# A last network in scaled float16 parts for passes 2 to 4, its last steps held behind the next pair of experts, and a planner that models port and clock

## The chip, the cores and the metric

The kernel runs on one core of one Trainium2 chip. The metric is device time in microseconds (us), from launch to end. The program gives each engine its own stream of instructions, in a written order: TensorE (PE) multiplies matrices, with weight loads shown apart as PEld; VectorE (DVE), ScalarE (ACT) and GpSimd (POOL) work element by element; SyncE (SP) issues most DMAs.

## The reference, cut to what matters

Three networks follow one another, all in float32; float64 stands for no output, but the last network's weights arrive as float64 words.

```python
a = softmax(where(sink or in window, q @ k.T / 8, -1e9)) @ v     # 2 x 8 heads, 768 positions, 64 wide
x = a as 1536 tokens x 512

flat = (x @ w_gate).flatten()                  # 8 experts, room for 192 tokens each
for idx in argsort(-flat):                     # greedy: best pair first
    tok, e = idx // 8, idx % 8
    if not taken[tok] and counts[e] < 192: assign tok to e
out[mask_e] = maximum(x[mask_e] @ w1[e], 0) @ w2[e]     # 512 -> 1024 -> 512, per expert

h = out @ w_in                                 # 512 -> 2048
g = maximum(h, 0) + alpha * minimum(h, 0)
return g @ w_out                               # 2048 -> 512
```

## The kernel before, in words

Attention runs first, to about 115 us of the profiled span. The greedy assignment then runs in eight phases, s = 0 to 7. Each fills one expert: comparisons `cm` on DVE and ACT (L994, L998, L1003), counts on PE (`closing`, L1045), and the list of that expert's 192 tokens. Between phases the tokens still free are packed closer (`compact`: a prefix count on PE, L1154 and L1156, then scatters `cd` on POOL, L1180, and a load back into a shorter table L). A gather on POOL (`xg`, L1295) fetches each expert's token rows, PE turns them (L1308), and the expert's two layers run as products in float32 (L1369), with weights `raw` loaded from memory.

Experts are taken in four pairs. After pair g comes pass g of the last network over that pair's 384 tokens: sixteen steps f = 0 to 15. A step multiplies the tokens by one 512 x 128 tile of w_in (`lay1`, L1423, 384 columns), applies the leaky rectifier (t on ACT, L1436; v on DVE, L1439), and multiplies by one 128 x 512 tile of w_out (`lay2`, L1458, 3 x 512 columns). A float32 operand is held as a high and a low part of type fp32r (a rounded float32 word). Three products, high x high, high x low, low x high, are summed: 12 matmuls in `lay1`, 9 in `lay2`. `split` makes the two parts of a weight tile (high on ACT, L1333; low on DVE, L1324), and does it again in each pass that uses the tile; x and g are split too (L1399, L1401; L1443, L1324). The first three steps of pass 1 are plain float32 (`FLAT1`, `FLAT2`; L1429). The text counts passes from 1, the code counts g from 0.

The 32 weight tiles come as pairs of 32-bit words and are turned into float32 during pair 1 and pass 1 (`Weights.convert`: ACT L796, DVE L798 and L800, then a sign from ACT L804 multiplied in on POOL L807). They stay in SBUF. A pass ends with an eviction from PSUM (L1492) and a scatter of its rows to `out` by POOL (L1496).

The order on every engine is written by `Plan`, a list scheduler. Each task carries an estimated duration; a task's rank is its longest way to the end. The planner takes what can start first by its own clock, with rank to break ties, and so decides before the run how phases, experts and passes are interleaved. The order is then fixed, whatever happens on the chip.

Of the kernel before, what the change touches and what calls it, by code (L numbers as in the profile page):

```python
# [74 lines left out]
class Task:  # L75
    __slots__ = ("eng", "fn", "deps", "succ", "left", "start", "end", "rank", "bufs", "tail", "n", "behind", "nbytes", "est", "by", "boost", "pre", "bias")


class Plan:
# [3 lines left out]
    HOP, SAME, BIAS = 0.2, 0.06, 0.85  # L83

    def __init__(self):
        self.tasks, self.soft, self.free = [], [], {}
        self.dma_free = 0.0

    def task(self, eng, fn, r=(), w=(), behind=None, after=(), tail=0.0, boost=0.0, nbytes=0, pre=None, bias=None):
# [3 lines left out]
        t = Task()  # L93
        t.eng, t.fn, t.tail, t.boost, t.n = eng, fn, tail, boost, len(self.tasks)
        deps = set(after)
# [36 lines left out]

    def run(self):
# [20 lines left out]
        while count:  # L154
            best = None
            for e, c in ready.items():
                at = self.free.get(e, 0.0)
                pick = None
                for t in c:
                    s, asked = max(at, t.est[e]), []  # L160
# [25 lines left out]
            self.free[e] = s + t.eng[e]  # L186
# [552 lines left out]
class Weights:  # L739


    LATE = 6

    def __init__(self, tc, nc, plan, ctx, w_in, w_out, alpha, wide, early):
# [4 lines left out]
        self.x, self.res, self.order, self.tasks = {}, {}, [None], []  # L749
        self.room(ctx, 0, early)  # L750
        cst = ctx.enter_context(tc.tile_pool(name="w_al", bufs=1))
        al, self.way, self.slope = [cst.tile([128, FB], F32, name=n) for n in ("al", "way", "slope")]
        al_res, self.way_res = Res(), Res()

# [10 lines left out]
    def room(self, ctx, a, b):  # L765
        pool = ctx.enter_context(self.tc.tile_pool(name=f"w_cst{a}", bufs=1))
        for n in range(a, b):
            self.x[n] = pool.tile([128, DM], F32, name=f"w{n}")
            self.res[n] = Res()

    def convert(self, a, b):
        nc, plan = self.nc, self.plan
        for n in range(a, b):
            f, s = divmod(n, 2)
            src, x, res = self.src[s][:, f], self.x[n], self.res[n]
            if not self.wide:
                plan.task({"SP": 0.06}, lambda x=x, src=src: nc.sync.dma_start(out=x, in_=src), w=[res],
                          nbytes=1 << 18)
                if s:
                    self.tasks.append(plan.task({"DVE": dve(DM // 2)}, lambda x=x, f=f: nc.vector.tensor_scalar(  # L780
                        x, x, self.way[:, f:f + 1], None, OP.mult), r=[self.way_res], w=[res]))
# [10 lines left out]
            def bits(k, r=r, x=x, sg=sg, f=f, s=s):  # L792
                lo, hi = words(r)[:, :, 0], words(r)[:, :, 1]
                b = x.bitcast(U32)
                if k == 0:
                    nc.scalar.activation(x, hi.bitcast(F32), AF.Copy, scale=2.0 ** -112)  # L796
# [9 lines left out]
            def signed(e, x=x, sg=sg):  # L806
                (nc.gpsimd if e == "POOL" else nc.vector).tensor_tensor(x, x, sg.tile, OP.mult)  # L807
# [3 lines left out]
            self.tasks.append(plan.task({"DVE": dve(DM // 2)}, lambda f=bits: f(1), w=[res]))  # L811
            plan.task({"DVE": dve(DM)}, lambda f=bits: f(2), r=[r], w=[res])
            if apart:
                plan.task({"ACT": act_sb(DM)}, lambda f=bits: f(4), r=[r, self.way_res] if s else [r], w=[sg])
                self.tasks.append(plan.task({"POOL": pool(DM), "DVE": dve(DM)}, signed, r=[sg], w=[res]))
            else:
                self.tasks.append(plan.task({"DVE": dve(DM)}, lambda f=bits: f(3), r=[r], w=[res]))
# [21 lines left out]
class Routed:  # L839
# [6 lines left out]
    LEAD = 0  # L846
# [73 lines left out]

    def name(self, ei, k, x, key):
# [8 lines left out]
    def closing(self, s, st, groups, r_bank, hold=(), fetched=False):  # L930
# [15 lines left out]
        for a, b in groups:  # L946
# [12 lines left out]
            if fetched:  # L959
# [4 lines left out]
                     r=[m.part(a)], w=[ps], after=hold)  # L964
# [5 lines left out]
            for x in range(a, b, 4) if not fetched else ():  # L970
# [11 lines left out]
                task({"PE": 0.11 * k}, bcast, r=[m.part(a)], w=[ps], after=hold)  # L982
# [5 lines left out]
            for a1, b1 in done:  # L988
                for c1 in range(a1, b1):
# [39 lines left out]
                    for k, x, y, op in sides:  # L1029
# [9 lines left out]
                        seq.append(task({"DVE": us}, fn, r=() if via else rr, w=cut[-1:]))  # L1039
                    counted.append(cnt.part(len(counted)))  # L1040

                    def count(c1=c1, cm=cm, lo=lo, b=b):
                        begun.append(c1)
                        for c in range(lo, b):
# [5 lines left out]
                         after=hold)  # L1050
# [24 lines left out]
        seq.append(task({"PE": 0.12}, lambda: total(0), r=[red, *counted], w=[cnt.part("t")]))  # L1075
        seq.append(task({"DVE": 0.25}, lambda: total(1), r=[cnt.part("t")], w=[tot]))
        seq.append(task({"PE": 0.12}, lambda: total(2), r=[tot], w=[cnt.part("b")]))
# [17 lines left out]
    def build(self, ctx, w1, w2, weights, out):  # L1095
# [23 lines left out]
        weights.r64.more(wrk, self.MORE)  # L1119
# [478 lines left out]
```

## Time and profile before

| | us |
|---|---|
| median of 3 runs | 651.32 (649.09 to 655.09) |
| profiled execution, whole | 645.53 |
| profiled execution, span | 643.8 |
| PE busy in it | 592.1 (92%) |
| PE weight loads | 510.5 (79%) |
| DVE busy | 399.0 (62%) |
| ACT busy | 321.0 (50%) |
| POOL busy | 172.8 (27%) |

The span runs from the first to the last instruction. A busy PE is counted from the start of a matmul to its modelled end, so steps overlap; the time that a matmul costs in a dense run is from its start to the next one's start. The mean granted TensorE clock is 0.962 of full speed. Passes and pairs of the profiled execution lie as follows: pass 1 to about 285 us, pair 2 to 333, pass 2 to 407, pair 3 to 453, pass 3 to 524, pair 4 to 571, pass 4 to 636, and the last stores to 644.

### The profile page before, as it was taken

What the parts mean: (1) busy time and instruction counts of PE and PEld (TensorE: products, weight loads), DVE (VectorE), ACT (ScalarE), POOL (GpSimd) and SP (SyncE); (2) the same over time, 40 slices, a digit from 0 to 9 for tenths busy, and PEclk for the clock granted to TensorE, in tenths of its full rate; (3) what the DMA queues carried; (4) which work ended last, traced back from release to release, by engine and by line L of the source; (5) the groups of instructions that cost most, each with busy time, mean ns of one, the idle gap of its engine ahead of it and who ended that gap; (6) DMA issues with size and microseconds to landing.
All of it is one profiled execution on the core that took longest, in us unless ns stands there. A gap on an engine that the chain in (4) does not pass through costs nothing.

```text
span 643.8 us, 11469 instructions
## 1 busy us (share of the span) xinstructions
PE 592.1 (92%) x4227; PEld 510.5 (79%) x4228; DVE 399.0 (62%) x1112; ACT 321.0 (50%) x670; POOL 172.8 (27%) x257
## 2 busy tenths in 40 slices
PE   6689996589799988989999999999999998999995
PEld 3466775359697777869999987899998888999994
DVE  4798999889578999863026587500656830035551
ACT  5688887345467885431225544311554441235552
POOL 4676726153384442131024011210000121000001
PEclk9999998569899999989999999999999999999998
DMA  7966344156887630516510005464000336600001
GB/s 216 278 132 134 98 85 129 57 203 205 319 271 226 202 130 1 176 53 212 180 49 5 0 25 182 147 193 135 26 2 0 135 104 190 202 1 1 1 1 49
DMA packets 41216, 76.53 MB, mean 119 GB/s; under 512 B 16324, under 2 KB 23016, under 8 KB 41064
## 3 DMA queue, kind: packets, MB, share of 16 engines
q1 hardware_dynamic: 38376, 68.87, 35.1%
q0 software_dynamic: 2784, 6.93, 3.2%
q8 instruction: 33, 0.54, 0.4%
q14 instruction: 23, 0.19, 0.1%
HBM read 66.75 MB, written 6.42 MB: 114 GB/s over the span
## 4 chain that ended last, share of the span: by engine, by line
PE 64%; DVE 15%; DMA 11%; issue 3%; POOL 3%; ACT 2%; SPq 1%; POOLq 0%; DVEq 0%; ACTq 0%
PE h L1369 19%; PE o L1458 16%; PE h L1423 16%; DMA xg<-xd,sidx 4%; PE s L459 3%; DVE cm L998 2%; PE pt L494 2%; DMA xT<-x 2%; DMA vraw<-v 2%; PE r L1308 2%; DVE spl L1324 2%; POOL cd L1180 2%; DVE w L798 1%; DVE w L800 1%; DVE cm L1013 1%
## 5 line engine op out<-in xcount | busy, mean ns | idle before, releaser
L1458 PE MATMUL o<-spl,gt 128*128 128x512 f32 x549 | 141.6, 400 | 0.9 <-DVE gt L1324 0.9
L1423 PE MATMUL h<-x,spl 128*128 128x384 f32 x732 | 138.0, 338 | 1.2 <-DVE spl L1324 1.2
L1423 PEld LDWEIGHTS h<-x,spl 128*128 128x128 f32 x732 | 128.3, 188 | 6.8 <-DVE spl L1324 1.5
L1324 DVE TENSOR_TENSOR spl<-w,spl 128x512 fp32r<-128x512 f32 x121 | 87.3, 722 | 55.3 <-ACT spl L1333 55.1
L1333 ACT CAST spl<-w 128x512 fp32r<-128x512 f32 x122 | 75.5, 619 | 87.3 <-PE o L1458 49.7
L1458 PEld LDWEIGHTS o<-spl,gt 128*128 128x128 f32 x549 | 101.0, 190 | 20.5 <-DVE gt L1324 1.5
L1369 PE MATMUL h<-xT,raw 128*128 128x192 f32 x512 | 91.7, 336 | 0.0
L1369 PEld LDWEIGHTS h<-xT,raw 128*128 128x128 f32 x512 | 85.3, 195 | 0.7 <-ACT h L1383 0.3
L1369 PE MATMUL h<-h,raw 128*128 128x192 f32 x512 | 85.8, 327 | 0.0
L1369 PEld LDWEIGHTS h<-h,raw 128*128 128x128 f32 x512 | 83.2, 190 | 0.3 <-issue 0.2
L1401 DVE TENSOR_TENSOR x<-h,x 128x192 fp32r<-128x192 f32 x32 | 11.3, 356 | 102.1 <-ACT x L1399 101.9
L1295 POOL DMA_INDIRECT xg<-xd,sidx x16 | 19.6, 1225 | 165.3 <-DVE sidx L1291 122.7
L1383 ACT ACTIVATE h<-h 128x192 f32<-128x192 f32 x64 | 21.1, 330 | 55.3 <-PE h L1369 55.3
L480 ACT ACTIVATE P<-sm,mn 128x260 f32<-128x260 f32 (+1 forms) x96 | 43.0, 490 | 8.1 <-DVE mn L469 7.3
L1439 DVE SCALAR_TENSOR_TENSOR v<-h,way,t 128x384 f32<-128x384 f32 x61 | 37.2, 611 | 12.8 <-ACT t L1436 12.8
L1436 ACT ACTIVATE t<-h,slope 128x384 f32<-128x384 f32 x64 | 37.0, 579 | 14.9 <-PE h L1423 14.2
L469 DVE CUSTOM_DVE_ANT_0 sm<-s,mask 128x260 f32<-128x260 f32 (+1 forms) x96 | 35.4, 398 | 8.4 <-PE s L459 7.5
L807 POOL TENSOR_TENSOR w<-w,sg 128x512 f32<-128x512 f32 x23 | 29.6, 1289 | 40.5 <-DVE w L800 22.1
L1443 ACT CAST gt<-v 128x384 fp32r<-128x384 f32 x61 | 31.1, 511 | 17.9 <-DVE v L1439 16.5
L459 PE MATMUL s<-k,q 64*128 64x260 f32 (+1 forms) x192 | 35.0, 455 | 4.7 <-DMA q<-qT 4.7
L998 DVE TENSOR_SCALAR cm<-mrow,m 128x384 bf16<-128x384 f32 (+8 forms) x75 | 37.3, 535 | 1.1 <-ACT mrow L983 1.1
L1399 ACT CAST x<-h 128x192 fp32r<-128x192 f32 x32 | 10.3, 322 | 53.8 <-PE h L1369 53.8
(207 smaller groups left out, 845.4 us busy)
## 6 DMA issues: line engine op xcount, KB each, us to landing
raw<-w SPq DMA_DIRECT2D x64, 512.0 KB, 3.8
r<-w_in SPq DMA_DIRECT2D x16, 512.0 KB, 3.6
r<-w_out SPq DMA_DIRECT2D x16, 512.0 KB, 3.7
vraw<-v SPq DMA_DIRECT2D x4, 768.0 KB, 11.5
xd<-x SPq DMA_DIRECT2D x12, 256.0 KB, 2.0
k<-kT SPq DMA_DIRECT2D x11, 260.0 KB, 6.1
q<-qT SPq DMA_DIRECT2D x11, 256.0 KB, 2.8
mrow<-md SPq DMA_DIRECT2D x2, 576.0 KB, 6.0
```

The lines of the kernel that those rows point to most:

```text
L459: nc.tensor.matmul(s.tile[:, :n], lhsT=qs[t].tile[half, p], rhs=kk, start=True, stop=True)
L469: task({"DVE": dve(n)}, lambda: nc.vector.tensor_tensor_reduce(out=sm.tile[:, :n], in0=s.tile[:, :n], in1=mask[:, :n], scale=-0.125, scala ...
L480: task({"ACT": act(n) + 0.137}, lambda h=h, sm=sm, mn=mn: nc.scalar.activation(P[t].tile[:, h, :n], sm.tile[:, :n], AF.Exp, bias=mn.tile, ...
L998: nc.vector.tensor_scalar(cm.tile[:, x:y], mrow[:, x:y], m.tile[:, c1:c1 + 1], None, op)
L1324: eng.tensor_tensor(*aps(), OP.subtract)
L1333: (nc.scalar.copy if e == "ACT" else nc.vector.tensor_copy)(b.tile[:, 0], get())
L1369: nc.tensor.matmul(ps.tile[:, 0:CAP], lhsT=w[:, k], rhs=x, start=first and k == 0, stop=last and k == 3, skip_group_check=True)
L1423: nc.tensor.matmul(ps.tile[:, 0:CH], lhsT=w[:, i, k], rhs=y[:, j], start=(k == n == 0), stop=(k == KD - 1 and n == 2))
L1436: task({"ACT": act(CH)}, lambda: nc.scalar.activation(t.tile, ps.tile[:, 0:CH], AF.Copy, scale=slope), r=[ps, weights.way_res], w=[t])
L1439: task({"DVE": dve(CH) + 0.065}, lambda: nc.vector.scalar_tensor_tensor(to(), ps.tile[:, 0:CH], way, t.tile, OP.mult, OP.max), r=[ps, t, w ...
L1443: task({"ACT": act_sb(CH)}, lambda: nc.scalar.copy(gt.tile[:, 0], v.tile), r=[v], w=[gt.part(0)])
L1458: nc.tensor.matmul(ops[t].tile, lhsT=gt.tile[:, i, sl], rhs=wo.tile[:, j], start=(f == n == 0), stop=(f == FB - 1 and n == 2))
```

## The change

**Float16 parts.** Passes 2 to 4 hold their operands as two float16 parts of the operand times a power of two. `bounds` takes the largest magnitude of each of the 32 weight tiles (an `Abs` activation with an accumulator on ACT, L808, or a reduction on DVE, L810), joins them by two small transposes on PE (L820, L823), and forms the factors (L827 to L834). `halve` then makes the parts of each tile once, in a ring of 34 buffers: high on ACT (L856), low on DVE (L861). Passes 2 to 4 all use them; no weight tile is split again. For x the factor is formed per expert: magnitudes off PSUM (L1508), two transposes (L1515, L1519), small steps (L1524 to L1532), then two highs on ACT (L1542) and two lows on DVE (L1544). The eviction multiplies by `kt` to take the factors out again. Pass 1 keeps fp32r.

**Held steps.** `chunk` returns `finish`, which writes the last two steps' `lay2`, the eviction and the store. For passes 1 to 3 it is called after the next pair of experts has been written down.

**Planner.** `port` lets no two marked tasks of DVE and POOL overlap in the plan; `stream` doubles the planned time of PE work in a window in which it takes the clock to be low; `urge` adds 300 to the rank of small PE steps of phases s >= 2 and of the new chains. Estimates of a float16 step are 1.95 and 0.65 in place of 2.08 and 0.69.

```diff
-    def task(..., pre=None, bias=None):
+    def task(..., pre=None, bias=None, urge=0.0, port=False):
+        t.port = {"DVE": port, "POOL": not tail}
+    def stream(self, s, us):
+        k = int(s / self.WINDOW)
+        while len(self.warm) <= k:
+            n = len(self.warm) - 1
+            self.warm.append(self.work.get(n, 0.0) > self.WINDOW * (0.32 if self.warm[n] else 0.75))
+        us *= 1.0 if self.warm[k] else 2.0
...
+        for t in todo:
+            t.rank += t.urge
-                    s, asked = max(at, t.est[e]), []
+                    s, asked = max(at, t.est[e], self.port if t.port.get(e) else 0.0), []
-            self.free[e] = s + t.eng[e]
+            self.free[e] = s + (self.stream(s, t.eng[e]) if e == "PE" else t.eng[e])
+            if t.port.get(e):
+                self.port = self.free[e]
+    def bounds(self, r_bank, ident):
+        for n in range(2 * FB):
+            def bound(e, n=n, at=k * FB + f):
+                if e == "ACT":
+                    nc.scalar.activation(self.junk, x, AF.Abs, accum_out=mx[:, at:at + 1])
+                else:
+                    nc.vector.tensor_reduce(mx[:, at:at + 1], x, AX.X, OP.max, apply_absolute_value=True)
+            plan.task({"ACT": 0.8, "DVE": 0.69}, bound, r=[self.x[n]], w=[res[n]])
...
+    def halve(self):
+        for n in range(2 * FB):
+            def high(e, x=x, v=view, k=k):
+                if e == "ACT":
+                    nc.scalar.activation(v()[:, 0], x.tile, AF.Copy, scale=self.rise[:, k:k + 1])
...
+            def low(x=x, v=view, k=k):
+                nc.vector.scalar_tensor_tensor(v()[:, 1], x.tile, self.rise[:, k:k + 1], v()[:, 0], OP.mult, OP.subtract)
+    def urge(self, s):
+        return 0.0 if s < 2 else 300.0
-            seq.append(task({"PE": 0.028 * nb}, prefix, r=[al], w=[ps]))
+            seq.append(task({"PE": 0.028 * nb}, prefix, r=[al], w=[ps], urge=300.0))
-                wi = None if flat else split(lambda: x[0], [x[1]])
+                wi = weights.h[2 * f] if half else None if flat else split(lambda: x.tile, [x])
-                    for k in range(KD):
-                        y = x2.tile[:, k]
-                        for n, (i, j) in enumerate(((0, 0), (0, 1), (1, 0))):
+                    ways = [(k, i, 0) for k in range(KD) for i in range(2)] + [(k, 0, 1) for k in range(KD)]
+                    for n, (k, i, j) in enumerate(ways):
...
-            for t in range(TB):
-                ot = (r_ot if g < E // 2 - 1 else r_raw).new()
+            def finish():
+                if g < E // 2 - 1:
+                    for p in pend:
+                        lay2(*p)
+                for t in range(TB):
+                    ot = (r_ot if g < E // 2 - 1 else r_raw).new()
...
+        finish = lambda: None
+        for g in range(E // 2):
+            xf, kt = r_xf.new(), r_kt.new() if g else None
+            x2 = [r_x2.new() for _ in range(1 if g else 2)]
+            expert(2 * g, x2, xf, kt)
+            expert(2 * g + 1, x2, xf, kt)
+            finish()
+            finish = chunk(g, x2, xf, kt)
+            if not g:
+                weights.bounds(r_r, ident)
+                weights.halve()
+        finish()
```

The order of the instructions moves at three places. Names: `alive` are the tokens still free, `upper` and `ones` the matrices of the prefix count, `ohs` the one-hot rows of expert 1's list, `xg` its gathered rows.

PE, around the prefix count that packs the tokens before phase 2; first before, where it stands behind the turning of expert 1's rows:

```order
L1369 MATMUL h_3286<-h_3169,raw_3171 128x192
L1308 MATMUL r_3319<-ident,xg_3281 128x64
L1308 MATMUL r_3319<-ident,xg_3292 128x128
L1308 MATMUL r_3319<-ident,xg_3281 128x64
L1308 MATMUL r_3319<-ident,xg_3292 128x128
L1308 MATMUL r_3327<-ident,xg_3281 128x64
L1308 MATMUL r_3327<-ident,xg_3292 128x128
L1308 MATMUL r_3327<-ident,xg_3281 128x64
L1308 MATMUL r_3327<-ident,xg_3292 128x128
L1154 LDWEIGHTS upper
L1154 MATMUL r_3337<-alive_3251,upper 128x12
L1156 LDWEIGHTS ones
```

and now, where the turning (L1410 of the changed kernel) comes 55 instructions later:

```order
L1378 LDWEIGHTS ohs_2730
L1378 MATMUL r_3218<-tok,ohs_2730 128x1
L1256 LDWEIGHTS upper
L1256 MATMUL r_3242<-alive_3227,upper 128x12
L1258 LDWEIGHTS ones
L1258 MATMUL r_3242<-alive_3227,ones 128x11
```

The count moved ahead of the step that needs the gathered rows, and into the indexing of expert 1's list.

PE, from pair 2 to pass 2; first before, where `lay1` of pass 2 follows the next prefix count:

```order
L1156 LDWEIGHTS ones
L1156 MATMUL r_4841<-alive_4645,ones 128x2
L1156 LDWEIGHTS ones
L1156 MATMUL r_4841<-alive_4645,ones 128x1
L1423 MATMUL h_4858<-x_4689,spl_4345 128x384 x12
L1423 MATMUL h_4875<-x_4689,spl_4356 128x384 x12
```

and now, with the held steps of pass 1 (L1622, parts `spl`) and the two chains of factors (`wm`, `wtop` of the weights, `xm`, `tm` of expert 3's x):

```order
L1471 MATMUL h_4837<-h_4812,raw_4810 128x192
L820 MATMUL r_4869<-ident,wm_2696 3x128
L1622 MATMUL o_3671<-spl_4560,gt_4563 128x512 x3
L1515 MATMUL h_4837<-ident,xm_4827 4x128
L1622 MATMUL o_3690<-spl_4560,gt_4563 128x512 x3
L1519 MATMUL h_4837<-ident,tm_4883 128x4
L823 MATMUL r_4869<-ident,wtop 128x3
L1622 MATMUL o_3709<-spl_4560,gt_4563 128x512 x3
L1622 MATMUL o_3671<-spl_4617,gt_4612 128x512 x3
L1622 MATMUL o_3690<-spl_4617,gt_4612 128x512 x3
L1622 MATMUL o_3709<-spl_4617,gt_4612 128x512 x3
L1579 LDWEIGHTS w_4921
```

Eighteen held matmuls and four small transposes stand between the last product of pair 2 and the first float16 step, L1579.

DVE, at the start of pass 2, in the changed kernel; before, rows of `spl` (L1324) alternate with v and the low part of g there:

```order
L834 TENSOR_TENSOR wsc<-wsc 128x1
L1544 SCALAR_TENSOR_TENSOR x_4761<-xf_4699,xs_4890,x_4761 128x2x192 x2
L861 SCALAR_TENSOR_TENSOR w_4921<-w_2709,wsc,w_4921 128x512
L861 SCALAR_TENSOR_TENSOR w_4926<-w_2713,wsc,w_4926 128x512
L839 TENSOR_SCALAR way_2700<-way,wsc 128x16
L840 TENSOR_SCALAR slope_2701<-slope,wsc 128x16
L861 SCALAR_TENSOR_TENSOR w_4945<-w_3048,wsc,w_4945 128x512
L861 SCALAR_TENSOR_TENSOR w_4951<-w_2711,wsc,w_4951 128x512
```

The factors, the lows of x and the first lows of the weights stand in one row there; all 32 lows of the weights lie in pass 2, and none in passes 3 and 4.

## Rows read from the trace of the kernel before

**Rows 1.** Busy time by stretch: us, then busy time (instructions) of PE, PEld, DVE, ACT, POOL.
```profile
142.00:200.00 58.00, 54.29 (x419) 50.92 (x416) 43.96 (x107) 32.66 (x71) 28.37 (x35) 0.92 0.74 248
200.00:240.00 40.00, 39.08 (x168) 29.88 (x167) 39.44 (x59) 32.20 (x57) 19.43 (x15) 1.00 0.60 186
240.00:285.50 45.50, 39.88 (x295) 31.91 (x294) 37.53 (x100) 21.05 (x40) 10.88 (x10) 0.96 0.20 69
285.50:332.90 47.40, 46.99 (x325) 44.84 (x324) 11.77 (x44) 10.13 (x29) 4.56 (x8) 1.00 0.51 162
332.90:406.80 73.90, 72.41 (x412) 63.03 (x411) 51.80 (x125) 36.78 (x71) 16.50 (x24) 1.00 0.15 47
406.80:452.60 45.80, 45.80 (x294) 43.78 (x294) 8.71 (x37) 10.04 (x29) 4.37 (x6) 1.00 0.54 167
452.60:523.90 71.30, 71.30 (x392) 62.50 (x391) 46.68 (x108) 36.97 (x70) 2.49 (x4) 1.00 0.12 42
```
**Rows 2.** Waits of PE from 142 us on, by stretch in order: us, times, longest.
```profile
PE r L1308 <- DMA xg<-xd,sidx: 3.3, 2, 3.0
...
PE r L1308 <- DMA xg<-xd,sidx: 3.2, 1, 3.2
PE h L1423 <- DVE spl L1324: 1.2, 1, 1.2
...
PE r L1308 <- DMA xg<-xd,sidx: 1.2, 1, 1.2
...
PE r L1308 <- DMA xg<-xd,sidx: 1.7, 1, 1.7
```
**Rows 3.** Timeline of PE in pass 3: start, us, engine, line.
```profile
481.52 2.24 PE L1423 MATMUL h<-x,spl 128*128 128x384 f32 x12
483.60 2.22 PE L1458 MATMUL o<-spl,gt 128*128 128x512 f32 x9
485.66 2.24 PE L1423 MATMUL h<-x,spl 128*128 128x384 f32 x12
```
**Rows 4.** Timeline of PE in attention: a run of twelve float16 matmuls.
```profile
39.89 0.19 PE L545 MATMUL pv<-vh,pth 128*128 128x65 f16 x1
...
40.22 0.19 PE L549 MATMUL pv<-vh,ptl 128*128 128x65 f16 x1
```
**Rows 5.** Groups by line and form, pass 3: busy us, mean ns.
```profile
L1324 DVE TENSOR_TENSOR spl<-w,spl 128x512 fp32r<-128x512 f32 x31 | 21.3, 688 | 17.1 <-ACT spl L1333 17.1
L1333 ACT CAST spl<-w 128x512 fp32r<-128x512 f32 x31 | 19.2, 620 | 26.1 <-PE o L1458 13.6 <-PE h L1423 12.5
```
**Rows 6.** Groups by line and form, to 130 us; the last row from 142 to 243 us.
```profile
L601 ACT ACTIVATE x<-x,scv 128x512 f16<-128x512 f32 x10 | 7.2, 720 | 1.5 <-DVE x L572 1.4
L381 ACT ACTIVATE junk<-vraw 128x512 f32<-128x512 f32 x4 | 2.5, 626 | 2.1 <-DMA vraw<-v 2.1
L381 ACT ACTIVATION_READ_ACCUMULATOR junk<-vraw 128x1 f32 x4 | 0.7, 186 | 0.0
L383 DVE TENSOR_REDUCE mx<-vraw 128x1 f32<-128x512 f32 x8 | 5.1, 678 | 1.1 <-DMA vraw<-v 1.1
L416 DVE SCALAR_TENSOR_TENSOR vl<-vraw,scv,vh 128x512 f16<-128x512 f32 x1 | 0.8, 760 | 0.0
L798 DVE TENSOR_SCALAR w<-w 128x512 uint32<-128x512 uint32 x1 | 0.4, 418 | 0.0
...
L798 DVE TENSOR_SCALAR w<-w 128x512 uint32<-128x512 uint32 x29 | 16.5, 576 | 3.0 <-ACT w L796 2.9
```
**Rows 7.** Timeline of DVE and PE around the packing before phase 2.
```profile
164.31 0.17 DVE L1159 TENSOR_SCALAR alive<-dead 128x12 bf16<-128x12 f32 x1
176.41 0.17 DVE L1162 SCALAR_TENSOR_TENSOR pos<-dead,r 128x12 f32<-128x12 f32 x1 [4.58 <-PE r L1156]
...
173.50 2.58 PE L1308 MATMUL r<-ident,xg 128*128 128x128 f32 x7 [3.03 <-DMA xg<-xd,sidx]
175.87 0.22 PE L1154 MATMUL r<-alive,upper 128*128 128x12 bf16 x1
```

More of the change, by code (lines that the diff above doesn't have):

```diff
@@ L75 @@
 class Task:
-    __slots__ = ("eng", "fn", "deps", "succ", "left", "start", "end", "rank", "bufs", "tail", "n", "behind", "nbytes", "est", "by", "boost", "pre", "bias")
+    __slots__ = ("eng", "fn", "deps", "succ", "left", "start", "end", "rank", "bufs", "tail", "n", "behind", "nbytes", "est", "by", "boost", "pre", "bias", "urge", "port")
 class Plan:
@@ L131, in seen @@
         return d.end + (self.SAME if d.by == e else self.HOP)
+    def stream(self, s, us):
[4 more added lines that the diff above has]
+        us *= 1.0 if self.warm[k] else 2.0
+        e = s + us
+        while s < e:
+            x = min(e, (k + 1) * self.WINDOW)
+            self.work[k] = self.work.get(k, 0.0) + max(0.0, x - s)
+            s, k = max(x, s), k + 1
+        return us
     def run(self):
@@ L763, in __init__, with room @@
         self.ways = lambda: plan.task({"DVE": 0.2}, ways, r=[al_res], w=[self.way_res])
[L765 to L769, printed above, removed]
+    def room(self, ctx):
+        self.ring = Ring(ctx.enter_context(self.tc.tile_pool(name="w_cst", bufs=1)), "w", [128, DM], F32, 2 * FB + self.MORE)
+        self.x = {n: self.ring.new() for n in range(2 * FB)}
@@ L845 @@
     V = 3
-    LEAD = 0
+    RISE = 300.0
     YIELD = 2.5
@@ L1333, in high @@
                 (nc.scalar.copy if e == "ACT" else nc.vector.tensor_copy)(b.tile[:, 0], get())
-            last_split[0] = task({"ACT": act_sb(512), "DVE": dve(256)}, high, r=reads, w=[b.part(0)],
+            last_split[0] = task({"ACT": act_sb(512), "DVE": dve(256)}, high, r=reads, w=[b.part(0)], port=True,
                                  behind=last_split[0])
@@ new lines, in expert @@
+            if kt is None:
+                return
+            tm, xs, w16 = r_tm.new(), r_xs.new(), x2[0]
+            spare = lambda: ps.tile[0:KD, 256:384]
+            task({"PE": 0.12}, lambda: nc.tensor.transpose(spare(), xm.tile[:, 0:KD], ident),
+                 r=[xm.part(d) for d in range(KD)], w=[ps.part("t")], urge=up)
+            task({"DVE": 0.28}, lambda: nc.vector.tensor_reduce(tm.tile, spare(), AX.X, OP.max), r=[ps.part("t")], w=[tm],
+                 urge=up)
+            task({"PE": 0.12}, lambda: nc.tensor.transpose(ps.tile[:, 400:400 + KD], tm.tile.to_broadcast([KD, 128]),
+                                                           ident[0:KD, 0:KD]), r=[tm], w=[ps.part("b")], urge=up)
@@ L1406, in chunk, with gview @@
+        def chunk(g, x2, xf, kt):
             ops = [r_o.new() for _ in range(TB)]
             both = [(d, a) for d in range(KD) for a in range(2)]
-            xr = [x2.part((d, x, a)) for d, a in both for x in range(2)] if x2 is not None else []
-            xfr = [xf.part(k) for k in both] if xf is not None else []
+            half = kt is not None
+            if half:
+                xr = [[x2[0].part((k, x, a)) for k in range(0, KD, 2) for a in range(2)] for x in range(2)]
+            else:
+                xr = [[x2[x].part(k) for k in both] for x in range(2)]
+            xfr = [xf.part(k) for k in both]
+            def gview(gt):
+                return gt.tile[:, 0].bitcast(F16).rearrange("p (a t) -> p a t", a=2)
@@ L1447, in second @@
             def second(f, gt, wo):
-                x = weights.x[2 * f + 1], weights.res[2 * f + 1]
-                wo.append(x if (g, f) in self.FLAT2 else split(lambda: x[0], [x[1]]))
+                x = weights.x[2 * f + 1]
+                wo.append(weights.h[2 * f + 1] if half else x if (g, f) in self.FLAT2 else split(lambda: x.tile, [x]))
             def lay2(f, gt, w, ts=range(TB)):
```

257 lines of the change are left out of this document (172 added, 85 removed).

## The prediction

> **What bounds the kernel now.** I read the busy time by stretch first, then the waits of PE, then PE's timeline inside a pass, and last the groups that give prices.
>
> The stretches show a kernel that PE bounds nearly everywhere after 142 us [rows 1]. In pass 3 (452.6 to 523.9 us) PE is busy for all 71.3 us at full granted clock, while DVE has 46.7 and ACT 37.0 us of work. Pass 2 is the same but for 1.5 us. Only pass 1 is different: from 200 to 285.5 us DVE is busy 39.4 + 37.5 = 77.0 of 85.5 us and PE 79.0, so two engines are nearly full at once. ACT has 53.3 there. Idle PE from 142 to 332.9 us sums to 3.7 + 0.9 + 5.6 + 0.4 = 10.6 us. The waits say what ended it [rows 2]: mostly the turning of gathered rows behind its DMA, only 1.2 us on a weight split. So a shorter split saves nothing by itself in passes 2 to 4; a shorter matmul does.
>
> A step there is a fixed pattern [rows 3]: 12 matmuls of 384 columns from 481.52 to 483.60, 2.08 us or 173.3 ns each, and 9 of 512 from 483.60 to 485.66, 2.06 us or 228.9 ns each. Columns at the full clock of 2.4 GHz would be 160.0 and 213.3 ns, so each fp32r matmul has 13 to 15 ns on top.
>
> **Float16 steps.** The nearest float16 rows are in attention [rows 4]: twelve matmuls of 64 or 65 columns, each with its own weight load, start from 39.89 to 40.22, eleven gaps of 30 ns. 64.5 columns at 2.4 GHz are 27 ns, so 3 ns are on top, and the loads are hidden even behind so short a matmul. For 384 and 512 columns I add the same 3 ns: 163 and 216.3 ns. A step saves 12 x 10.3 + 9 x 12.6 = 124 + 113 = 237 ns; 16 steps in 3 passes make 11.4 us. Bounds: nothing, if long float16 matmuls carry the fp32r rows' 13 to 15 ns, and 48 x (0.16 + 0.14) = 14.4 us if nothing is on top. I take 11.4, since the float16 rows are the same type and form.
>
> The Trainium skill, TensorE: Matmul & The Clock Gate, section "Wait — 56ns, not 53.3ns?", gives N ÷ 2.4 GHz plus about 2.5 ns from start to start once the clock is up. If that held for every type, the fp32r steps would already take 162.5 and 215.8 ns and nothing could be saved; the fp32r rows of this trace are 11 to 13 ns above it, so for them it does not hold.
>
> **Splits and halves.** A pass now loses 32 splits, 0.688 us on DVE and 0.620 on ACT each [rows 5]; both lie beside PE, so their loss is worth nothing in passes 3 and 4. In their place pass 2 alone has 32 lows on DVE at 0.760 us, the price of the same form in attention, and 32 highs on ACT at 0.720 [rows 6]. DVE's work in pass 2 is then 51.8 - 22.0 + 24.3 = 54.1 us, plus the closing of phase 5 that moves in from the experts' stretch (8.7 us there [rows 1]): 62.8, and up to about 71 where each row of the new order is priced by its group. PE has 72.4 - 3.8 = 68.6 us there. So DVE and PE are nearly level and DVE may end last now and then: 0 to 4 us, I take 1.0. ACT, with 36.8 - 19.8 + 23.0 = 40 us, stays beside.
>
> **Maxima in pass 1.** Thirty go to ACT at 0.626 + 0.186 = 0.81 us, 24.4 us in all, and two to DVE at 0.68 [rows 6]. ACT rises to 53.3 + 24.4 = 77.7 of 85.5 us: it is covered, with 8 us to spare. DVE gets 1.4 us and the closing of phase 3, some 9 of the 11.8 us that DVE has in the next stretch, in place of small work that leaves it: 77.0 + 1.4 + 9 = 87.4 against 85.5. That alone would make pass 1 end 2 us later, and 6 if DVE again leaves 5% of its time unused.
>
> **Routing put earlier.** Against this stands the prefix count before phase 2. The free tokens are known at 164.31 us, but the count runs at 175.87, because on PE it stands behind the turning, which waits 3.03 us for gathered rows; DVE waits 4.58 us behind it [rows 7]. In the new order it stands ahead of the turning. The scatters and the table of phase 2 can come up to 11 us earlier, and the later gathers too. What this can give is not 11 us but at most PE's idle time up to pass 2, 10.6 us, and some of that has other releasers; 6 is my upper bound. I set the whole of pass 1 and pair 2 at 0, with -6 and +6 as ends. In passes 2 to 4 two waits for gathered rows, 1.2 and 1.7 us [rows 2], should go: -2.9, or nothing.
>
> **Held steps and the chains.** After the last product of pair 2 the first float16 step needs a chain: a reduction off PSUM (between 0.17 us of a short DVE row [rows 7] and 0.68 of a 512-wide one [rows 6], say 0.35), a transpose of about 0.22, a reduction 0.2, a transpose 0.22, then twelve small DVE rows at 0.17, x's lows 0.76, the first tile's high and low 0.72 + 0.76: 5.3 us, with hand-overs about 6.4. The 18 held matmuls cover 18 x 0.229 = 4.1 us. PE then idles 2.3 us; ends 0 and 6.4. Before passes 3 and 4 the weights' part is absent, about 3.5 us against 4.1 of cover, so nothing. The price is also a gain given up: held steps are the same work, only later. The evictions and stores behind them run beside `lay1` of the next pass, which needs no such PSUM bank for four steps, 8 us. POOL's three stores stand behind nine scatters there; I count that as hidden. The tail behind pass 4 stays, its eviction only scaled.
>
> **Sum.** 645.5 (the profiled execution) - 11.4 + 1.0 + 0 - 2.9 + 2.3 = 634.5 us. The median shown is 651.3, 5.8 above the profiled execution, and a new time will be a median too: **640.3**, said as 640.
>
> **Rivals.**
>
> *Routing gives its full bound.* PE's idle time before pass 2 goes down by 6 us and the maxima cost nothing: 634. For it speaks the 11.6 us between the free tokens and the count; against it that DVE is nearly full in pass 1 anyhow. Chance 0.14.
>
> *The gain is eaten before pass 2.* Pass 1 ends 6 us later because DVE has more there, pass 2 is paced by DVE for another 3, and the cover at the first boundary is 2 short: 640 + 11 = 651, no change. For it speaks DVE's 77 of 85.5 us. Chance 0.17.
>
> *Float16 steps are no shorter.* 640.3 + 11.4 = 652, no change: then the change does not do what its estimates say. The attention rows speak against it. Chance 0.05.
>
> *Slower: DVE's rows lengthen beside POOL.* One DVE form, L798, took 0.418 us in a quiet stretch and 0.576 on the mean where POOL converts [rows 6], 1.38 times. Place: DVE from 200 us to the end of pass 2, where late conversion, scatters and halves now meet. Price: lows of weights 32 x 0.29 = 9.3 us, and 12% of pass 1's 88 us, 10.5: 640 + 20 = 660. It decides once the lows take more than about 0.9 us, for then pass 2's DVE work is above PE's. Against it: POOL has only 16.5 us of work in pass 2 [rows 1], fewer with the splits gone. Chance 0.12.
>
> The Trainium skill, SBUF — State Buffer, section "SBUF: two separate sides", says that a DVE instruction with two SBUF inputs and a GpSimd one that reads SBUF exclude each other for a whole instruction, and the lows have two such inputs. By that rule POOL's descriptor writing and signs would wait behind them too. The L798 rows agree that the two get in each other's way, though L798 has one input; no row here shows the wait of POOL itself.
>
> **The numbers.** The forecast has 0.52. A change under 1%, 6.5 us, can't be told from none: below 644.8 is faster, above 657.8 slower. Faster: 0.50 of the forecast and 0.14 of the first rival, 0.64. Same: 0.02 of the forecast, 0.14, 0.05 and 0.03 of the last three, 0.24. Slower: 0.03 of the second rival and 0.09 of the fourth, 0.12. The range goes from 627 (float16 at its bound of 14.4, and routing's 6 us, with a little more from the boundary) to 655 (pass 1 at +6, pass 2 at +4 and the boundary uncovered, half the float16 gain); it leaves out most of the slower case and little else.
>
> **What the profile will show.** Steps of passes 3 and 4 at 1.96 and 1.95 us from start to start, or 2.08 and 2.06 if float16 is no shorter. Pass 2's first `lay1` at about 333 us: earlier means that routing gave more, later that DVE or the chain costs more, and the wait named there tells which. In pass 2 waits of PE on the halves (L861), few or many. Lows at 0.76 us, or near 1. The count L1256 at about 165 us. I would be wrong in kind if passes 3 and 4 were not shorter by about 4 us each, and wrong in size most likely by what pass 1 does.

## The result

The changed kernel took 630.21 us (median of 4 runs, 628.55 to 630.84) beside 650.21 for the kernel before (647.13 to 655.09): a ratio of 0.972, 95% interval 0.967 to 0.976. Two later comparisons, each beside runs of the kernel before on the same chip, gave 0.979 (0.974 to 0.984) and 0.973 (0.968 to 0.978). The forecast was 640, 1.7% less; the change brought 2.8%. The profiled execution took 629.71 us, its span is 628.0 at a mean clock of 0.961, against 645.53, 643.8 and 0.962 before: 15.8 us by profiles, 20 by medians.

Busy time by stretch in the kernel after, cut where its passes and pairs begin; columns as in [rows 1], and behind the busy times the granted clock, the share of DMA time and GB/s:

```profile
142.00:200.00 58.00, 51.97 (x415) 49.13 (x414) 43.04 (x111) 40.44 (x93) 24.34 (x33) 0.89 0.74 247
200.00:240.00 40.00, 39.02 (x235) 27.90 (x234) 37.18 (x93) 31.44 (x65) 12.39 (x10) 1.00 0.51 174
240.00:283.00 43.00, 42.76 (x284) 35.72 (x283) 39.99 (x94) 29.21 (x62) 13.39 (x10) 1.00 0.32 97
331.40:397.90 66.50, 65.25 (x420) 35.28 (x421) 58.39 (x160) 38.95 (x71) 13.85 (x18) 1.00 0.19 63
441.90:512.20 70.30, 70.12 (x417) 37.07 (x416) 31.59 (x95) 23.11 (x45) 7.11 (x10) 1.00 0.18 61
554.10:620.20 66.10, 66.10 (x355) 34.50 (x354) 21.68 (x43) 21.79 (x40) 4.07 (x7) 1.00 0.03 13
```

PE is now full in pass 1 too (busy 42.8 of its last 43 us, where it was 39.9 of 45.5), but ahead of 200 us it idles 6.0 of 58 us, where it idled 3.7. Its weight loads in passes 2 to 4 have fallen to about half of the time, and DVE is nearest to PE in pass 2, as forecast, but below it. Where the time came from is read from the starts of the passes' first `lay1`; before:

```profile
332.72 3.54 PE L1423 MATMUL h<-x,spl 128*128 128x384 f32 x19
452.39 6.48 PE L1423 MATMUL h<-x,spl 128*128 128x384 f32 x36
570.27 6.04 PE L1423 MATMUL h<-x,spl 128*128 128x384 f32 x33
```

and now (pass 2's, at 331.41, stands among the rows of the boundary below):

```profile
446.38 3.90 PE L1579 MATMUL h<-x,w 128*128 128x384 f16 x23
558.58 3.74 PE L1579 MATMUL h<-x,w 128*128 128x384 f16 x22
```

Pass 4 ends at 636.0 before and 620.2 now. So 1.3 us came ahead of pass 2, 4.7 in pass 2 and pair 3, 5.7 in pass 3 and pair 4, 4.1 in pass 4; the tail of 7.8 us is the same. The first of these is no more than executions differ by: pass 2 began at 335.2 in a second profile of the kernel before, and at 335.6 and 330.3 in two more of the changed kernel. From pass 2's start to the end of the span the profiles stand apart: 311.1 and 310.4 us before; 296.6, 301.6 and 296.7 now.

Steps of pass 4 after, on PE's timeline (compare [rows 3]):

```profile
576.11 2.10 PE L1622 MATMUL o<-w,gt 128*128 128x512 f16 x9
578.05 2.11 PE L1579 MATMUL h<-x,w 128*128 128x384 f16 x12
580.00 2.11 PE L1622 MATMUL o<-w,gt 128*128 128x512 f16 x9
```

From start to start 1.94 and 1.95 us in place of 2.06 and 2.08. The boundary ahead of pass 2, on PE's timeline of the kernel after:

```profile
326.20 0.27 PE L820 MATMUL r<-ident,wm 128*3 128x128 f32 x1
326.23 0.95 PE L1622 MATMUL o<-spl,gt 128*128 128x512 f32 x3
328.14 0.19 PE L823 MATMUL r<-ident,wtop 3*128 3x3 f32 x1
328.27 3.01 PE L1622 MATMUL o<-spl,gt 128*128 128x512 f32 x12
331.41 0.34 PE L1579 MATMUL h<-x,w 128*128 128x384 f16 x1
332.20 7.81 PE L1579 MATMUL h<-x,w 128*128 128x384 f16 x47 [0.45 <-DVE w L861]
339.85 2.10 PE L1622 MATMUL o<-w,gt 128*128 128x512 f16 x9
342.74 2.10 PE L1622 MATMUL o<-w,gt 128*128 128x512 f16 x9 [0.79 <-ACT ot L1664]
```

The same stretch on DVE's timeline:

```profile
326.40 0.36 DVE L1508 TENSOR_REDUCE xm<-h 128x1 f32<-128x192 f32 x1 [0.87 <-PE h L1471]
329.88 1.14 DVE L1544 SCALAR_TENSOR_TENSOR x<-xf,xs,x 128x384 f16<-128x384 f32 x2
331.39 1.42 DVE L861 SCALAR_TENSOR_TENSOR w<-w,wsc,w 128x512 f16<-128x512 f32 x2 [0.37 <-ACT w L856]
```

The chain ran from 326.4 to 332.1; held matmuls filled PE to 331.3, and 0.45 us of waiting was left. The second wait is new: the third eviction needs a buffer (`ot`) that a store still holds, and that store stands behind nine scatters on POOL.

### The profile page after: what moved, and what is told of

Its sections match the earlier page's. It is cut to its first block, busy times and chain, and to the rows that moved or that the text cites. A ratio compares the mean times of both kernels' runs of the same rounds, so it can differ in the third digit from the quotient of the medians.

```text
span 628.0 us, 11487 instructions
## 1 busy us (share of the span) xinstructions
PE 581.8 (93%) x4240; PEld 428.6 (68%) x4242; DVE 368.2 (59%) x1131; ACT 315.2 (50%) x681; POOL 160.7 (26%) x246
## 4 chain that ended last, share of the span: by engine, by line
PE 68%; DMA 10%; DVE 9%; ACT 5%; POOL 3%; issue 2%; SPq 1%; POOLq 0%; DVEq 0%; ACTq 0%
PE h L1471 21%; PE o L1622 16%; PE h L1579 16%; DMA xg<-xd,sidx 3%; PE s L481 3%; PE pt L516 3%; DMA vraw<-v 2%; PE r L1410 2%; DVE cm L1097 2%; POOL cd L1282 2%; ACT cm L1102 1%; DMA xT<-x 1%; DVE cm L1112 1%; PE r L1144 1%; DMA L<-cd 1%
## 5 line engine op out<-in xcount | busy, mean ns | idle before, releaser
L1622 PE MATMUL o<-w,gt 128*128 128x512 f16 x432 | 103.2, 379 | 0.8 <-ACT ot L1664 0.8
L1579 PE MATMUL h<-x,w 128*128 128x384 f16 x576 | 100.5, 326 | 0.6 <-DVE w L861 0.5
L1579 PEld LDWEIGHTS <-w 128*128 128x128 f16 x576 | 56.0, 98 | 41.8 <-DVE w L861 0.7
L1622 PEld LDWEIGHTS <-gt 128*128 128x128 f16 x432 | 40.4, 98 | 42.6 <-issue 1.4
L1508 DVE TENSOR_REDUCE xm<-h 128x1 f32<-128x192 f32 x24 | 8.6, 358 | 101.6 <-PE h L1471 101.6
L903 POOL TENSOR_TENSOR w<-w,sg 128x512 f32<-128x512 f32 x23 | 32.9, 1430 | 77.7 <-DVE w L896 50.3
L502 ACT ACTIVATE P<-sm,mn 128x260 f32<-128x260 f32 (+1 forms) x96 | 42.8, 490 | 3.1 <-DVE mn L491 2.4
L1668 POOL DMA_INDIRECT out<-ot,sidx x9 | 9.6, 1066 | 133.0 <-ACT ot L1659 131.8
L1496 ACT COPY xf<-h 128x192 f32<-128x192 f32 x32 | 10.2, 318 | 58.0 <-DVE xm L1508 55.9
L1599 ACT CAST gt<-v 128x384 f16<-128x384 f32 x48 | 24.4, 509 | 25.7 <-DVE v L1595 24.1
L1600 DVE TENSOR_TENSOR gt<-v,gt 128x384 f16<-128x384 f32 x48 | 26.7, 555 | 16.6 <-ACT gt L1599 16.4
```

The lines of the kernel that those rows point to most:

```text
L502: task({"ACT": act(n) + 0.137}, lambda h=h, sm=sm, mn=mn: nc.scalar.activation(P[t].tile[:, h, :n], sm.tile[:, :n], AF.Exp, bias=mn.tile, ...
L903: (nc.gpsimd if e == "POOL" else nc.vector).tensor_tensor(x.tile, x.tile, sg.tile, OP.mult)
L1579: nc.tensor.matmul(ps.tile[:, 0:CH], lhsT=w[:, i, k], rhs=y[j][:, k], start=(n == 0), stop=(n == len(ways) - 1))
L1599: task({"ACT": act_sb(CH)}, lambda: nc.scalar.copy(gview(gt)[:, 0], v.tile), r=[v], w=[gt.part(0)])
L1600: task({"DVE": dve(CH) + 0.1}, lambda: nc.vector.tensor_tensor(gview(gt)[:, 1], v.tile, gview(gt)[:, 0], OP.subtract), r=[v, gt.part(0)], ...
L1622: nc.tensor.matmul(ops[t].tile, lhsT=gv[:, i, sl], rhs=wv[:, j], start=(f == n == 0), stop=(f == FB - 1 and n == 2))
```

## Experiments

The first set (before_again, no_half, no_hold, no_plan) ran beside a kernel before of 646.9 us, the second (after_again, fill, only_half, no_max) 649.7, the third (fill2, no_urge, after_third, spare) 648.4. Ratios are to these.

**before_again**: no edit.

> The kernel before, unchanged, profiled once more. Its profiled execution took 645.5 us while its timed runs had a median of 650.2 (647.1 to 655.1); the changed kernel's profiled execution and median agree within 0.5 us. Theory: the executions of the kernel before differ by several us among themselves, in waits for DMA ahead of 333 us, so this one's span may come out anywhere from 644 to 653, and where it differs from the first one its steps in passes 3 and 4 are the same 2.08 and 2.06 us and the difference lies in named waits for gathered rows or loads. Rival: the profiled execution is shorter than the timed runs by some 5 us because of the profiling, then this one is near 645 again and its timed runs near 650.

Measured: ratio 0.9995 (0.995 to 1.004), span 645.6 us. Its runs lie between 642.1 and 650.4, with the profiled execution inside them; steps are the same. So the 5.8 us that the prediction added from the first profiled execution to the median were no property of profiling: this kernel's runs differ by that much among themselves.

**no_half**

```diff
-            xf, kt = r_xf.new(), r_kt.new() if g else None
-            x2 = [r_x2.new() for _ in range(1 if g else 2)]
+            xf, kt = r_xf.new(), None
+            x2 = [r_x2.new() for _ in range(2)]
...
-            if not g:
-                weights.bounds(r_r, ident)
-                weights.halve()
```

> The changed kernel without float16: passes 2 to 4 split their weights in each pass as before, no maxima, no halves; held steps and the planner's rules stay. Theory: float16 steps save 237 ns each, 11.4 us of the 15.8 by which the profiled spans differ, the rest being waits that the planner's order removed; so this kernel comes to 630.2 + 11.4 = 641.6, 639 to 645, and steps of 2.08 and 2.06 us return in its passes 3 and 4. Rival: the order and the held steps made most of the gain and float16 little; then it stays at 634 or below. Other rival: the float16 parts also freed DVE and ACT enough to matter; then it comes to 648 or above.

Measured: 645.0 us, at the upper end of the theory's 639 to 645, ratio 0.997 (0.993 to 1.002), the same as the kernel before; span 641.9. Pass 4 of it on PE's timeline:

```profile
599.85 2.22 PE L1622 MATMUL o<-spl,gt 128*128 128x512 f32 x9
601.91 2.25 PE L1579 MATMUL h<-x,spl 128*128 128x384 f32 x12
604.00 2.22 PE L1622 MATMUL o<-spl,gt 128*128 128x512 f32 x9
```

The steps are back at 2.06 and 2.09 us. Without float16 the rest of the change is worth nothing that can be measured. By spans float16 carries 13.9 us, where the steps explain 11.4. The order differs too: the first held step starts at 331.25 us in place of 326.23, 5.0 us later, and from there on the kernel loses 8.9. These two parts were not taken apart further.

**no_hold**

```diff
-            finish()
-            finish = chunk(g, x2, xf, kt)
+            chunk(g, x2, xf, kt)()
```

> The changed kernel with the last two steps, the eviction and the stores of a pass written directly behind the pass, not behind the next pair. Theory: the 18 held matmuls cover the chain of factors before passes 2 to 4, 4 to 5 us each time; without them PE waits about 5 us before pass 2 and 3 us before passes 3 and 4, 11 us less what the planner finds as other cover, so 634 to 641. Rival: the planner fills the gap with other work and the held steps are worth nothing, 629 to 632.

Measured: 649.8 us, ratio 1.0045 (1.001 to 1.008): 8 us and more above both theories, and 0.4% slower than the kernel before, although all its float16 steps are there. The boundary ahead of pass 3 and what follows, on this kernel's PE timeline:

```profile
452.55 0.27 PE L1515 MATMUL h<-ident,xm 128*4 128x128 f32 x1 [0.69 <-ACT xf L1496]
453.20 0.21 PE L1519 MATMUL h<-ident,tm 4*128 4x4 f32 x1 [0.37 <-DVE tm L1517]
454.94 3.61 PE L1579 MATMUL h<-x,w 128*128 128x384 f16 x12 [1.52 <-ACT x L1542]
460.82 3.44 PE L1579 MATMUL h<-x,w 128*128 128x384 f16 x12
482.17 3.66 PE L1579 MATMUL h<-x,w 128*128 128x384 f16 x12
```

Its busy time by stretch there (columns as above):

```profile
455.00:458.60 3.60, 3.59 (x13) 1.51 (x12) 1.52 (x4) 0.40 (x2) 0.00 (x0) 0.58 0.30 114
460.80:464.20 3.40, 3.40 (x19) 1.77 (x20) 3.31 (x10) 0.51 (x1) 0.00 (x0) 0.59 0.00 0
482.00:485.70 3.70, 3.70 (x14) 1.73 (x15) 0.00 (x0) 0.48 (x1) 2.02 (x3) 0.55 0.39 90
485.70:530.00 44.30, 44.30 (x236) 23.21 (x235) 12.95 (x22) 12.88 (x24) 0.00 (x0) 1.00 0.02 5
```

PE waits 0.69 + 0.37 + 1.52 = 2.6 us for the chain, close to the 3 us of the theory. Then the granted clock is 0.58, near the lower level of 1.2 GHz, and a step takes 3.61 us in place of 1.95; behind small waits for comparisons, and again behind a wait of 1.2 us for gathered rows, it is as low. The same follows the other two boundaries (0.52 and 0.55). A wait is thus paid twice, with 1.66 us lost on the first step behind 2.6 us of waiting. The Trainium skill, TensorE: Matmul & The Clock Gate, section "HAM oscillation — how this bites in real kernels", tells of a kernel that waits for a DMA before each tile and so starts every tile at the low clock. This trace agrees in the effect (0.58 behind the waits), though the waits here are for ACT and DVE.

**fill**, on top of no_hold's edit:

```diff
+            if a:
+                spot, last = r_o.new(), main[-1]
+                for n in range(8):
+                    def idle(n=n):
+                        for k in range(3):
+                            nc.tensor.matmul(spot.tile[:, 0:CAP], lhsT=ident, rhs=xT.tile[:, k], start=True, stop=True)
+                    task({"PE": 0.49}, idle, r=halves, w=[spot], after=[last], urge=200.0)
```

> The kernel without held steps (which took 649.8 us, more than the kernel before), with 24 products of the second expert's x and the identity, 3.9 us, on PE ahead of passes 2 to 4 in the place of the held steps; their result goes nowhere. In that kernel PE idles 2.6 us at each of these boundaries, and float16 steps behind the idle time take 3.4 to 3.6 us in place of 1.95. Theory: the held steps are worth so much because they keep PE at work, and so its clock up, while the chain of factors runs; then the filler, which does nothing useful, gains back the 1.5 to 3.3 us per boundary that the low clock costs and loses up to 1 us where it outlasts the chain: 641 to 646, with no step over 2.3 us behind a boundary. Rival: only the idle time counts and the low clock is of the order's making; then filler leaves the time at 649 to 652.

Measured: 656.0 us, ratio 1.012 (1.004 to 1.019), above both theories: the filler took 8.2 us at each boundary, since a float32 product with the identity is recorded as two matmuls, and so it was twice as long as meant. Still no step behind a boundary is slow, and from pass 3's first step to the next pair it is 69.6 us in place of no_hold's 77.3.

**fill2**: the same with `range(4)`.

> The filler once more at half its size: each product with the identity was recorded as two matmuls, so the first filler took 8.2 us at each boundary in place of the 3.9 meant. Without held steps pass 3 took 77.3 us from its first step to the next pair; with the long filler 69.6, with no slow step. Theory: the long filler was 12 to 13 us too long in all, so this one comes to 640 to 645, under the kernel without held steps (649.8, ratio 1.0045) and not far above the changed kernel; float16 steps behind the boundaries stay at 1.95 us. Rival: the filler itself delays something else and the kernel stays at 649 or above.

Measured: 644.6 us, inside the theory's 640 to 645, ratio 0.996 (0.992 to 0.9996), against 1.0045 without filler. Work that does nothing makes the kernel shorter by 0.9%, some 5.6 us. This kernel's PE timeline at the same boundary:

```profile
453.68 0.21 PE L1519 MATMUL h<-ident,tm 4*128 4x4 f32 x1
455.41 2.11 PE L1588 MATMUL h<-x,w 128*128 128x384 f16 x12 [1.52 <-ACT x L1551]
457.51 2.11 PE L1588 MATMUL h<-x,w 128*128 128x384 f16 x12
```

The stretch behind it:

```profile
455.40:459.40 4.00, 3.99 (x30) 2.49 (x30) 4.00 (x11) 1.50 (x3) 0.00 (x0) 1.00 0.00 0
```

The last wait of the chain, 1.52 us, is as long as without filler, yet the clock stays at 1.00: what went before it on PE made the difference. The held steps do the same with work that has to be done anyhow. What fill2 lacks against the changed kernel of its set, 15.3 us by spans, is about what three fillers (3.9 us of matmuls each) and its 3.9 us of waits at the boundaries come to: 0.9958 against 0.973.

**only_half**: no_hold and no_plan together.

> Float16 parts alone: held steps and the planner's three additions off. Without held steps the kernel took 649.8, without the planner's additions 641.3. Theory: the two losses lie in different places (boundaries of passes; phases 2 and 3 during pass 1), so they add: 630 + 20 + 12, 655 to 664, slower than the kernel before, though every float16 step is shorter. Rival: both have one cause, the same idle time, and it comes to 648 to 653.

Measured: 658.4 us, ratio 1.0095 (1.006 to 1.013): slower than the kernel before, as the theory had it. Ahead of pass 2 PE waits 3.26 us and then runs at a clock of 0.50, as the stretch in the last line shows:

```profile
347.70 0.50 PE L1579 MATMUL h<-x,w 128*128 128x384 f16 x1 [3.26 <-ACT w L856]
349.26 3.06 PE L1579 MATMUL h<-x,w 128*128 128x384 f16 x9 [1.06 <-DVE w L861]
347.70:353.00 5.30, 4.24 (x13) 1.89 (x14) 4.68 (x12) 2.66 (x4) 2.85 (x5) 0.50 0.01 1
```

Float16 parts alone are a loss of 1%, and with what surrounds them a gain of 2 to 3%. But the losses without held steps (3.2 points) and without the planner's rules (1.7) do not add up to this one (3.1 to 3.7 points): the sum would be a ratio of 1.022, and 1.0095 is nearer to the rival's 648 to 653 us, 1.002 to 1.009 by the first set. The two losses overlap; where, was not traced.

**no_plan**

```diff
-        t.port = {"DVE": port, "POOL": not tail}
+        t.port = {"DVE": False, "POOL": False}
-        us *= 1.0 if self.warm[k] else 2.0
+        us *= 1.0
-            t.rank += t.urge
+            t.rank += 0.0
```

> The changed kernel with the planner's three additions off: no shared port, no clock, no urge; float16 and held steps stay. Theory: the additions removed the two waits for gathered rows in passes 2 to 4 (2.9 us) and put the prefix count 11 us earlier, worth about 2 us before pass 2; without them 633 to 637, with those waits back and the count near 175 us. Rival: they moved the order without moving the time, 629 to 632. Other rival: without urge the chains of factors stand late on PE and each boundary costs more, 640 or above.

Measured: 641.3 us, ratio 0.990 (0.981 to 0.9985) from four runs. It loses some 11 us against the changed kernel, more than the 3 to 7 forecast, and comes out where the last rival, chains that stand late, put it. Its trace, of the longest of these runs, does not bear that rival out at every boundary: ahead of passes 3 and 4 PE does not wait, ahead of pass 2 it waits 0.9 and 1.4 us on the first tile's halves, and its longest wait, 4.3 us, is for a comparison in pass 1.

**no_urge**: the last of these edits alone.

> The changed kernel without urge alone; port and clock stay in the plan. Theory: of the 8 to 12 us that the planner's additions are worth, most lie in pass 1, where without them PE waited 4.3 us on a comparison of phase 3 and lost its clock behind it; urge moves those small steps, so this kernel loses 6 to 12 us against the changed one beside it. Rival: port and clock, which space the comparisons on DVE, made it; then no_urge stays within 3 us of the changed kernel.

Measured: ratio 0.992 (0.988 to 0.997) beside 0.973 for the changed kernel, a loss of 12 to 13 us, just above the theory's 6 to 12. That is as much as no_plan loses: without urge, port and clock bring nothing that can be told. Whether they bring something beside urge was not run, and no run shows whether the planner's model of the clock fits the chip. Pass 1 of no_urge, on PE's timeline:

```profile
246.31 0.26 PE L1144 MATMUL r<-oh,cm 128*128 128x8 bf16 x4 [2.10 <-DVE cm L1097]
246.92 3.88 PE L1579 MATMUL h<-x,spl 128*128 128x384 f32 x12
```

The stretch behind that wait, and one behind a wait of 2.3 us for gathered rows:

```profile
246.90:250.80 3.90, 3.90 (x23) 3.74 (x22) 3.07 (x10) 1.30 (x3) 0.00 (x0) 0.57 0.00 0
276.30:280.60 4.30, 4.30 (x19) 3.10 (x19) 0.86 (x2) 1.48 (x3) 0.00 (x0) 0.50 0.00 0
```

PE waits 2.10 us for a comparison of phase 3, then runs at 0.57. By 333.3 us it is 8.2 us behind the changed kernel of the same set (325.1), and loses 7.8 more in passes 2 and 3, where it waits 1.4 us on a half, 0.9 on another, 1.4 on a high part of g and 2.4 in all for gathered rows.

**no_max**

```diff
-            plan.task({"ACT": 0.8, "DVE": 0.69}, bound, r=[self.x[n]], w=[res[n]])
...
+            for at, val in ((3, 2.0 ** 17), (4, 2.0 ** 18), (5, 2.0 ** -25), (6, 2.0 ** 8), (7, 2.0 ** -18), (8, 2.0 ** 25)):
+                nc.vector.memset(o[:, at:at + 1].bitcast(F32), val)
```

> The changed kernel without the 32 maxima of the weights and their chain; the factors are written as constants that suit these inputs. Theory: the maxima lie beside PE on ACT and their chain under the held steps, so leaving them out gives 0 to 2 us: 627 to 630. Rival: ACT is what ends pass 1, and without its 24 us there the kernel gains 4 us or more, 626 or below.

Measured: 639.0 us, ratio 0.981 (0.975 to 0.988), beside 0.979 for the changed kernel in the same set: no gain. The test is not clean, for with the factors known early the planner put 31 of the highs ahead of 330 us, and pass 2 of this kernel waits longer on an eviction than any profile of the changed kernel:

```profile
351.67 0.81 PE L1592 MATMUL o<-w,gt 128*128 128x512 f16 x3 [2.71 <-ACT ot L1634]
352.31 3.79 PE L1549 MATMUL h<-x,w 128*128 128x384 f16 x12
```

The changed kernel's profile in the same set lost some 5 us near that place too (after_again, below), so a gain or a loss of a few us can't be read from this pair. What 24 us of maxima on ACT cost stays open.

**after_again** and **after_third**: no edit.

> The changed kernel, unchanged, beside the runs of the kernel before on the same chip as the others of this set. The first comparison gave a ratio of 0.972, while the kernel before has come out between 642 and 655 us in its runs. Theory: the same ratio, 0.970 to 0.976, some 628 to 631 us, and a second profiled span within 2 us of 628.0, since all its waits but a few lie ahead of 200 us.

> The changed kernel unchanged a third time, beside the version with other eviction buffers. Its two earlier profiled spans were 628.0 and 637.2 us; 5.0 of the 9.2 us lay between pass 2 and pass 3, the rest ahead of pass 2, none behind. Theory: its time depends on whether idle stretches near 350 us and ahead of 200 us leave PE's clock up or down, so this one comes to 628 to 639, and again passes 3 and 4 take the same time to within 0.5 us.

Measured: 638.3 and 629.2 us; spans 637.2 and 627.0. The first missed its theory (628 to 631, span within 2 us of 628.0), the second lies inside its own. From pair 4's end on, the three profiled executions agree within 0.1 us (73.8). The long one lost 4 us ahead of pass 2, and 5 in pass 2, here on PE's timeline:

```profile
347.23 1.21 PE L1622 MATMUL o<-w,gt 128*128 128x512 f16 x3 [1.70 <-ACT gt L1599]
349.20 4.00 PE L1622 MATMUL o<-w,gt 128*128 128x512 f16 x9 [0.77 <-ACT ot L1664]
353.00 3.07 PE L1579 MATMUL h<-x,w 128*128 128x384 f16 x12
```

The two slow steps as a stretch:

```profile
349.20:355.90 6.70, 6.70 (x21) 2.83 (x21) 4.83 (x11) 3.04 (x5) 0.97 (x1) 0.57 0.11 42
```

The wait for `ot` stands in all three, but only here, with 1.70 us of another wait just ahead of it, is the clock behind it 0.57, and two steps take 6.7 us from start to start in place of 3.9. That the time depends on whether the clock stays up near 350 us holds for these three; what differs ahead of 200 us was not traced.

**spare**

```diff
-                    ot = (r_ot if g < E // 2 - 1 else r_raw).new()
+                    ot = (r_spl if g < E // 2 - 1 else r_raw).new()
...
```

> The changed kernel with the evictions of passes 1 to 3 put into free buffers of the weight splits (five, unused from pass 2 on) in place of a ring of two. The order is the same but for the third eviction behind pair 2, which moves up 14 places on ACT and no longer waits for the first store, which stands behind nine scatters on POOL. Theory: that wait holds ACT 1.2 us, PE 0.8 us, and in one of two executions a wait of 1.7 more and two steps at the low clock, 3.1 us; so this kernel is 1 us shorter where the clock stayed up and 5 to 6 where it fell, a ratio to the changed kernel beside it of 0.991 to 0.999, with no wait on an eviction in pass 2. Rival: another wait, on the halves or on a low part of g, takes its place within the same few steps and the time stays, 0.999 to 1.002.

Measured: 629.0 us, ratio 0.973 (0.969 to 0.978), beside 0.973 for the changed kernel. The wait is gone, and from pass 2's first `lay1` to pass 3's it is 114.0 us in place of 115.0 and 115.1:

```profile
330.72 7.81 PE L1579 MATMUL h<-x,w 128*128 128x384 f16 x47 [0.45 <-DVE w L861]
338.37 4.05 PE L1622 MATMUL o<-w,gt 128*128 128x512 f16 x18
```

That is the 1 us forecast, too little for the medians to show; the 5 to 6 us for executions whose clock falls could not be tested, since none of this set's profiles fell there. It is not measurably better than the changed kernel.

## Why the prediction was right, and where its sizes were off

The range (627 to 655) held the time and the direction was right; the gain was 1.8 times the forecast, 20 us in place of 11. The mechanism, shorter steps on a full PE with the chains hidden, is the one that ran; several sizes were off, mostly to the same side. By its own steps:

- **Float16 steps, -11.4.** Right to 0.01 us per step: 1.95 and 1.94 came where 1.96 and 1.95 were forecast. Pass 4, where little else changed, is 4.1 us shorter, against 3.8 forecast. The 3 ns on top of each short float16 matmul of attention [rows 4] hold for long ones.
- **Waits for gathered rows, -2.9.** Both are gone: PE waits for none behind 331 us.
- **Boundary ahead of pass 2, +2.3.** Mis-sized: PE waits 0.45 us. The chain took 5.7 us, close to the 6.4, but the held stretch covered 5.1 rather than 4.1. Ahead of passes 3 and 4 nothing, as forecast.
- **DVE in pass 2, +1.0.** DVE rows have 58.4 us (62.8 forecast) in the 66.5 us of that stretch, the lows 0.743 us each; PE waits 0.5 us on them and no more.
- **Stores behind scatters, counted as hidden.** Not so: 0.8 us on every profile, and more where the clock falls behind it.
- **Pass 1 and pair 2, 0.** Between -3.5 and +1.8 us in the three executions, if the held steps, 4.1 us, are counted as done; a second profile of the kernel before is 2.4 us longer there than the first. DVE did not end pass 1: it has 77.2 us in the 83 from 200 to 283, where 87.4 in 85.5 were feared, and ACT 60.7, where 77.7 were forecast, in part because ACT has 7.8 us more than before from 142 to 200 us. The count stands at 164.1 us (165 forecast), and the next phase's table still came only 2.4 us earlier, at 198.30 us in place of 200.66 on DVE: the load back was issued 5 us earlier and then took 6.3 us to land, against 3.6 before. So of 11.8 us of an earlier count 9.4 were given back on the way: 3.7 before the first scatter (169.0 in place of 177.1, behind two gathers on POOL), 3.1 between the last scatter and the load, 2.6 in the landing. How much the earlier count brought PE no run shows by itself.
- **From the profile to the median, +5.8.** The term that failed most: 634.5 was forecast for a profiled execution and 629.7 came, which is one half of the miss; the other half is this shift. The kernel before has runs between 642 and 655 us, and its first profile was one of the short ones; the changed kernel's first median is 0.5 us from its profile. A difference between one profile and one median was carried over as if it were fixed. That it vanished is in part luck, for the changed kernel spreads as far, from 626 to 639 us over its three comparisons.

What the prediction left out is the clock: it counted a wait as its own length. The experiments show that a boundary without held steps costs its 2.6 us and then at least 1.7 us of a slow clock, 4.9 ahead of and in pass 3, and that the planner's urge, which I weighed for its 11 us of earlier start, is worth some 12 us. Without it come longer waits in pass 1 and later, and a low clock behind them. The forecast came out near because the change had both; float16 alone, which the largest term stood for, is slower than before (only_half). By the same pricing no_hold was expected at 634 to 641 us and came at 649.8, so the sum holds only for an order that leaves few waits, and that it met such an order is in part luck.

Of the rivals, slower beside POOL did not come: lows took 0.743 us, under the 0.9 that would decide. Routing's full bound did not come either, and the gain was not eaten before pass 2, which began no later than before in two of three profiles. The rival without shorter steps is excluded by the steps themselves.

## What to carry to other kernels

Shorter matmuls in a PE-bound stretch paid here only where the new preparation left no long hole on PE (0.973 with held steps, 1.0045 without). So hold back finished-but-unneeded matmuls (the last steps of the stretch before) and put them where the chain of factors runs. Price a wait on PE together with the clock behind it, from a stretch of the trace where that happened. And before adding a gap between profile and median to a forecast, look at the spread of the runs: both kernels here spread over 13 us, and one profile says little about where the median lies.

## What the runs showed of the hardware that was not expected

At the full clock a float16 matmul of 384 columns costs 162.5 ns from start to start and one of 512 columns 215.6; the fp32r ones of the same sizes cost 173.3 and 228.9 [rows 3], and no_half brings these back.

A step of twelve float16 matmuls takes 1.95 us at a granted clock of 1.00 and 3.4 to 3.7 at 0.55 to 0.59, and the fall can follow waits of 0.4 to 1.5 us in a row (no_hold). The same wait of 1.52 us is followed by a clock of 0.58 in one kernel and 1.00 in another whose PE had filler ahead of it; and the same kernel, behind the same wait of 0.8 us, keeps its clock in two executions and loses it in a third, in which a wait of 1.70 us stands just ahead, 5 us in all.
